# Memory-term loads two pieces ahead, its z vector only where it changes, and third-stage weights loaded three ahead

## The chip, the cores and the metric

The program runs on one NeuronCore of a Trainium2 chip. The metric is the device time of one execution in microseconds (us), shown as the median of three runs. A profiled execution of the same kernel gives the trace that the rows below are from.

## The reference

The inputs are q, k, v (4 batches x 8 heads x 576 tokens x 64), a memory matrix M per head (64 x 64), a vector z per head (64) and one gate value per head. Three stages follow one another:

```
a       = softmax(causal(q k^T / 8));  local = a v
qp      = phi(q),  phi(x) = x + 1 where x > 0, else exp(x)
mem     = (qp M) / (qp . z + 1e-6)
x       = g * mem + (1 - g) * local          g = sigmoid(beta), 2304 tokens x 512
x       = ((x w1) * (x w2)) w3 w_out         512 -> 1024 -> 1024 -> 512
h       = x w_in                             512 -> 2048
out     = (h - tanh(h)) w_out2               2048 -> 512
```

The weights arrive as 64-bit words and are decoded on the chip to fp32. Each matmul of the second and third stage is done three times over (high x high, high x low, low x high part of fp32), which is why a weight has a high and a low tile.

## The kernel before, in words

**First stage.** 16 head pairs, each in five blocks of queries: scores (`sc`), row maximum and exp (`st`, `p`), normalization on POOL, transposes (`t`, `g`), product with v (`o`), copied to the tiles `xs`. A background generator (`early`) is advanced a few steps per block: it folds w3 and w_out into one matrix (`fo`, `wf`), decodes the first weights of w1 and w2, and works on the memory term of the first group of tokens.

**Memory term.** The 2304 tokens are 18 pieces of 128, three to a group of 384. `mem_tok` works on one piece: load q (tile `mw`), min(q, 0) on DVE (L554), exp on ACT (L555), max(q, 0) plus that on DVE (L557), times z on POOL (L558), a reduction and a reciprocal on DVE (L561 to L564, tile `mst`), a scaling on POOL (L566), four transposes on PE (L570), and two copies to `mq` by the helper `copy`, which gives four in five to ACT (L438) and one to DVE (L440). `mem_mm` then multiplies `mq` by M, and DVE adds the result to `xs` (L587). z lies in one half of tile `mc` and is loaded anew for each piece (L552). Group 0 is worked on in the first stage, groups 1 to 5 in the second.

**Second stage.** Six groups g of 384 tokens, eight slices f each. For each (g, f): 24 matmuls with the weights `wa` and `wb` into two PSUM tiles `ab`; ACT copies one of them (`a`, L722); DVE multiplies (`a`, L723); ACT and DVE split the product into `abh` (L726) and `abl` (L727); 12 matmuls with `wf` for slice f - 1 (`x`). I write a(g,f) for the instruction of L723 of slice f of group g: it stands once per slice on DVE and serves as a clock of the stage. Between the slices steps of the memory term and of two decoders are put in. In group 0 the decoder `wd` supplies `wa` and `wb` slice by slice. After it the decoder `pre` takes the third stage's weights, in part: each of 24 pieces takes one load (L66), one ACT instruction (L74) and four DVE instructions (L75, L77, L81, L84), and ends in a tile named `z..p`. In group 5 a third decoder, `fd`, does the remaining eight pieces while the 24 are split into high and low.

A decoder has a width of two pieces being worked on at once, and a number `ahead` of pieces loaded or being worked on. The buffers of a load (`raw`) are three, those of the work (`T`) two.

**Third stage.** 96 slices: 12 matmuls (`h`), the function h - tanh(h) over ACT and DVE, 9 matmuls (`o`).

**Order.** The code yields between steps, and a scheduler in the build then puts the instructions of every engine and of the load queue (SP) in an order of its own. On the chip each engine runs its list in order, and so does SP: an instruction that waits holds up all behind it.

Of the kernel before, what the change touches and what calls it, by code (L numbers as in the profile page):

```python
# [11 lines left out]
F32 = mybir.dt.float32  # L12
# [5 lines left out]
AF = mybir.ActivationFunctionType  # L18
ALU = mybir.AluOpType
# [13 lines left out]
def block_kernel(ctx, tc, qk, qt, vt, mp, zp_d, beta, w1, w2, w3t, wo, wi, wo2, ident_d, mask_d, out):  # L33
    nc = tc.nc
    PE, DV, AC, PO, SP = nc.tensor, nc.vector, nc.scalar, nc.gpsimd, nc.sync
# [6 lines left out]
    zp = ctx.enter_context(tc.tile_pool(name="zp", bufs=1, side="right"))  # L42
# [104 lines left out]
    HIA, HF = 1, 1  # L147
# [7 lines left out]
    CLP = 0  # L155
# [19 lines left out]
    CPA = (0, 1, 3, 4)  # L175
# [125 lines left out]
    if True:  # L301
# [128 lines left out]
            AC.activation(out=dh, in_=src, func=AF.Copy)  # L430
            DV.tensor_tensor(out=dl, in0=src, in1=dh.bitcast(F32), op=ALU.subtract)

        ncopy = [0]

        def copy(dst, src, scale=None):
            ncopy[0] += 1
            if ncopy[0] % 5 in CPA:
                AC.activation(out=dst, in_=src, func=AF.Copy, scale=1.0 if scale is None else scale)  # L438
            elif scale is None:
                DV.tensor_copy(out=dst, in_=src)  # L440
            else:
                DV.tensor_scalar(out=dst, in0=src, scalar1=scale, scalar2=None, op0=ALU.mult)
# [56 lines left out]
        N = 384  # L499
# [19 lines left out]
        def ranges(t0, n):  # L519
            r = []  # L520
            t = t0
            while t < t0 + n:
                e = min(t0 + n, (t // 576 + 1) * 576)
                r.append((t - t0, e - t0, t // 576))
                t = e
            return r
# [7 lines left out]
        mem_t = {}  # L534

        def mem_setup():
            mem_t["c"] = zp.tile([128, 1024], F32, tag="z2", name="mc")
            mem_t["q"] = [zp.tile([128, 2, 512], F32, tag=f"z{3 + i}", name=f"mq{i}") for i in range(2)]
            mem_t["b"] = 0

        def mem_m(b):
            m = mem_t["c"][:, 512 + 256 * (b % 2):768 + 256 * (b % 2)]
            SP.dma_start(out=m.rearrange("p (a e) -> p a e", a=4), in_=mp[4 * b:4 * b + 4].rearrange("a p e -> p a e"))

        def mem_tok(g, tl):
            t0 = g * N + tl * 128
            w = zp.tile([128, 1024], F32, tag=f"z{tl % 2}", name="mw")
            qp, e_ = w[:, 0:512], w[:, 512:1024]
            SP.dma_start(out=qp, in_=qt[t0:t0 + 128])
            zb = mem_t["c"][:, 0:512]  # L550
            for a, e, b in ranges(t0, 128):
                SP.dma_start(out=zb[a:e], in_=zp_d[b:b + 1].squeeze(0).partition_broadcast(e - a))  # L552
            yield
            DV.tensor_scalar(out=e_, in0=qp, scalar1=0.0, scalar2=None, op0=ALU.min)  # L554
            AC.activation(out=e_, in_=e_, func=AF.Exp)  # L555
            yield
            DV.scalar_tensor_tensor(out=qp, in0=qp, scalar=0.0, in1=e_, op0=ALU.max, op1=ALU.add)  # L557
            PO.tensor_tensor(out=e_, in0=qp, in1=zb, op=ALU.mult)  # L558
            yield
            st = sm.tile([128, 24], F32, tag="mst", name="mst")  # L560
            DV.tensor_reduce(out=st[:, 0:8], in_=e_.rearrange("p (h d) -> p h d", h=8), axis=AX.X, op=ALU.add)  # L561
            DV.tensor_scalar(out=st[:, 8:16], in0=st[:, 0:8], scalar1=1e-6, scalar2=None, op0=ALU.add)
            DV.reciprocal(out=st[:, 16:24], in_=st[:, 8:16])
            DV.tensor_tensor(out=st[:, 0:8], in0=st[:, 16:24], in1=gates, op=ALU.mult)  # L564
            q3 = qp.rearrange("p (h d) -> p h d", h=8)
            PO.tensor_tensor(out=q3, in0=q3, in1=st[:, 0:8].unsqueeze(2).to_broadcast([128, 8, 64]), op=ALU.mult)  # L566
            yield
            t = ps["t"]()
            for hp in range(4):
                PE.transpose(t[:, hp * 128:hp * 128 + 128], qp[:, hp * 128:hp * 128 + 128], ident)  # L570
            for i in range(2):
                copy(mem_t["q"][i][:, :, tl * 128:tl * 128 + 128],
                     t[:, 256 * i:256 * i + 256].rearrange("p (a b) -> p a b", a=2))
            yield

        def mem_mm(g, i):
# [106 lines left out]
        pst.close()  # L683
        att.close()


        pools = {}
        for x in PO_:
# [17 lines left out]
        def ab_pe(xl, f):  # L706
            o = []
            for W in (W1, W2):
                p = psb.tile([128, 512], F32, tag="ab", name="ab")
                for k in range(4):  # L710
                    c = slice(k * 128, k * 128 + 128)
                    mm(p[:, 0:N], W[f][:, 0, c], xl[0][:, k], k == 0, False)
                    mm(p[:, 0:N], W[f][:, 0, c], xl[1][:, k], False, False)
                    mm(p[:, 0:N], W[f][:, 1, c], xl[0][:, k], False, k == 3)
                o.append(p)
            return o
# [3 lines left out]
        def ab_chain(g, f, o):  # L720
            a = b2.tile([128, N], F32, tag="a", name="a")
            AC.activation(out=a, in_=o[0][:, 0:N], func=AF.Copy)  # L722
            DV.tensor_tensor(out=a, in0=o[1][:, 0:N], in1=a, op=ALU.mult)  # L723
            h = b3.tile([128, N], F32R, tag="abh", name="abh")
            l = b3.tile([128, N], F32R, tag="abl", name="abl")
            AC.activation(out=h, in_=a, func=AF.Copy)  # L726
            DV.tensor_tensor(out=l, in0=a, in1=h[:].bitcast(F32), op=ALU.subtract)  # L727
            ab_t[g, f] = (h, l)
# [22 lines left out]
        def fslot(tag, dt=F32R):  # L751
            pool = zq if tag in ZX else xp if tag == "x0" else None
            return wslot(pool, tag, dt) if pool else slot(tag, dt)

        ftags = [*ZX, *ztags]
        NF = len(ftags)
        pre_t = {}

        def fin_src(j):
            f = j // 2  # L760
            return (wo2[f * 128:f * 128 + 128] if j % 2
                    else wi[:, f * 128:f * 128 + 128].rearrange("(k p) f -> p k f", p=128))

        def fin_item(j):
            def dst():
                t = fslot(free.popleft())
                fin_tiles[j] = t[:, 0], t[:, 1]
                return fin_tiles[j]

            return fin_src(j), dst  # L770

        def pre_item(j):
            def dst():
                i = j % NF
                if i not in pre_t:
                    pre_t[i] = fslot(ftags[i], F32)
                return pre_t[i][:, j // NF].bitcast(U32)

            return fin_src(j), dst
# [8 lines left out]
        def place(i, tags):  # L788
            for x, tag in enumerate(tags):
                t = fslot(tag)  # L790
                split(pre_t[i][:, x], t[:, 0], t[:, 1], DV if i % 3 == 2 else PO)
                fin_tiles[i + NF * x] = t[:, 0], t[:, 1]
            give([ftags[i]])

        wd = wdec[0]
        pre, fd, placed, left, plan = None, None, 0, [], list(PL)
# [3 lines left out]
        def give(tags):  # L800
            nonlocal given
            free.extend(tags)
            given += len(tags)
# [17 lines left out]
        for g in range(6):  # L821
            for f in range(8):
                wd.until(2 * f + 2)
                o = ab_pe(xl, f)
                ab_chain(g, f, o)
                if f >= 1:
                    x2_pe(g, f - 1)
                    if g == 5:
                        if f == 1:
                            pre.until(2 * NF)  # L830
                            fd = Decoder([fin_item(j) for j in range(2 * NF, 32)], 2, 2, PO if CLP else DV, False, HF)
                        left += [f"{x}{f - 1}" for x in ("wf", "wa", "wb")]
                        while plan and len(left) >= (2 if plan[0] == "P" else 1):
                            if plan.pop(0) == "P":
                                place(placed, [left.pop(0), left.pop(0)])
                                placed += 1
                            else:
                                give([left.pop(0)])
                    if g == 0:
                        wd.until(2 * f + 4)  # L840
                for _ in range(MS):
                    mem_step()
                if wd.done == 16:
                    if pre is None:
                        order = [*range(NZ), *range(NF, NF + NZ), *range(NZ, NF), *range(NF + NZ, 2 * NF)]
                        pre = Decoder([pre_item(j) for j in order], 2, 2, DV, True)
                    for _ in range(FS if g < 5 else FS5):
                        if pre.done < allowed:
                            pre.step()
                        elif fd and fd.done < given:  # L850
                            fd.step()
            if g + 1 < 6:
                mem_until(g + 1)
                xl = stage(g + 1)
            x2_pe(g, 7)
# [187 lines left out]
```

## Time and profile before

| | |
|---|---|
| time, three runs | 1062.58 us median (1062.35 to 1063.51) |
| profiled execution | 1063.58 us, its span 1061.8 us |
| mean granted TensorE clock | 0.976 of 2.4 GHz |
| PE matmul | 986.8 us busy, 93% of the span |
| PE weight loads | 862.6 us, 81% |
| DVE | 816.0 us, 77% |
| ACT | 614.4 us, 58% |
| POOL | 423.4 us, 40% |

Shares over the whole span hide that the stages have different limits. The first slice of the second stage reaches DVE at about 306 us, the second stage ends at about 657 us. A row is read from left to right: engine, line, operation, the tile that is written and those that are read; an idle time is put down to what ended it.

### The profile page before, as it was taken

The numbers are of one execution on the slowest core, as the hardware profiler recorded it, in microseconds if no ns is written. First come the engines' busy times: TensorE is split into PE (matmuls) and PEld (weight loads), VectorE is DVE, ScalarE is ACT, GpSimd is POOL, SyncE is SP. The second block draws the span as 40 slices with busy tenths as digits, with TensorE's granted clock in tenths as the row PEclk, the third lists the DMA queues.
The fourth block names the chain that finished last, engine by engine and source line by source line (L and its number), as shares of the span: only waits on it lengthen the run. The fifth ranks groups of instructions, "written<-read, shape, count | busy, mean of one in ns | idle before, by whom it ended". The sixth has DMA issues, their size and how long they took to land.

```text
span 1061.8 us, 15818 instructions
## 1 busy us (share of the span) xinstructions
PE 986.8 (93%) x5512; PEld 862.6 (81%) x5512; DVE 816.0 (77%) x1473; ACT 614.4 (58%) x1419; POOL 423.4 (40%) x432
## 2 busy tenths in 40 slices
PE   5799898978998898999999997999999999999998
PEld 3576666655687787999999997989999999999997
DVE  7989998999869998558221288788778788787776
ACT  5567677666732443334121444877777776776764
POOL 5888777777656422200000185322222222222221
PEclk9699999999999898999999999999999999999999
DMA  9764675552324454215000010000000000000000
GB/s 248 190 168 118 176 197 131 135 134 85 95 71 143 142 181 149 60 52 168 30 1 1 1 61 1 1 1 30 1 1 30 1 31 1 2 30 1 31 1 30
DMA packets 44415, 77.73 MB, mean 73 GB/s; under 512 B 5168, under 2 KB 30000, under 8 KB 42416
## 3 DMA queue, kind: packets, MB, share of 16 engines
q1 hardware_dynamic: 44336, 76.73, 25.7%
q8 instruction: 43, 0.70, 0.3%
q14 instruction: 36, 0.29, 0.1%
HBM read 72.00 MB, written 4.72 MB: 72 GB/s over the span
## 4 chain that ended last, share of the span: by engine, by line
PE 66%; DVE 21%; issue 4%; POOL 4%; ACT 2%; DMA 2%; SPq 0%; DVEq 0%; POOLq 0%; ACTq 0%
PE o L143 21%; PE h L143 19%; PE ab L143 13%; PE x L143 7%; DVE T L81 3%; DVE T L75 2%; PE sc L143 2%; POOL p L427 2%; DVE st L394 2%; DVE T L84 2%; PE fo L143 2%; DVE qs L224 2%; DVE T L77 2%; PE t L459 1%; DVE ks L226 1%
## 5 line engine op out<-in xcount | busy, mean ns | idle before, releaser
L925 POOL TENSOR_TENSOR gl<-s,gh 128x384 fp32r<-128x384 f32 x96 | 100.6, 1048 | 292.5 <-ACT gh L919 281.8
L427 POOL TENSOR_SCALAR p<-p,st 128x128 f32<-128x128 f32 (+2 forms) x144 | 111.7, 787 | 55.1 <-DVE st L420 25.8
L143 PE MATMUL x<-abh,wf 128*128 128x384 f32 x384 | 110.5, 349 | 4.1 <-ACT abh L726 4.1
L143 PE MATMUL ab<-xh,wa 128*128 128x384 f32 x384 | 110.3, 345 | 4.0 <-DVE a L723 2.0
L143 PE MATMUL ab<-xh,wb 128*128 128x384 f32 x384 | 108.4, 340 | 2.9 <-POOL wb L96 2.0
L143 PE MATMUL sc<-ks,qs 128*128 128x256 f32 (+4 forms) x384 | 91.7, 358 | 18.5 <-DVE qs L224 9.5
L407 ACT ACTIVATE p<-sc,st 128x256 f32<-128x256 f32 (+4 forms) x160 | 82.5, 527 | 32.6 <-DVE st L394 13.3
L901 DVE SCALAR_TENSOR_TENSOR s<-s,u 128x384 f32<-128x384 f32 x96 | 82.0, 855 | 22.0 <-ACT s L891 21.0
L723 DVE TENSOR_TENSOR a<-ab,a 128x384 f32<-128x384 f32 x48 | 26.4, 551 | 85.8 <-PE ab L143 73.0
L74 ACT ACTIVATE T<-raw 128x512 f32<-128x512 f32 x72 | 48.7, 677 | 67.8 <-POOL wa L99 14.0
L897 ACT ACTIVATE u<-u,pc 128x384 f32<-128x384 f32 x96 | 59.3, 619 | 43.6 <-DVE s L901 43.5
L143 PEld LDWEIGHTS sc<-ks,qs 128*128 128x128 f32 x384 | 63.0, 205 | 26.1 <-ACT p L407 10.1
L907 DVE TENSOR_TENSOR t<-h,t 128x384 f32<-128x384 f32 x96 | 53.3, 555 | 38.1 <-ACT t L890 37.7
L143 PEld LDWEIGHTS ab<-xh,wa 128*128 128x128 f32 x384 | 71.2, 191 | 8.8 <-issue 3.2
L143 PEld LDWEIGHTS x<-abh,wf 128*128 128x128 f32 x384 | 72.8, 195 | 5.3 <-ACT abh L726 5.0
L459 PE MATMUL t<-ident,p 128*128 128x128 f32 x320 | 54.7, 292 | 22.4 <-DVE g L440 8.1
L889 ACT ACTIVATE u<-h 128x384 f32<-128x384 f32 x96 | 47.0, 490 | 47.2 <-PE h L143 47.2
L143 PEld LDWEIGHTS ab<-xh,wb 128*128 128x128 f32 x384 | 71.2, 191 | 3.9 <-POOL wb L96 2.3
L143 PE MATMUL x<-abl,wf 128*128 128x384 f32 x192 | 67.9, 354 | 4.2 <-DVE abl L727 4.2
L906 DVE SCALAR_TENSOR_TENSOR s<-s,s 128x384 f32<-128x384 f32 x96 | 61.3, 638 | 8.5 <-DVE s L901 0.9
L143 PE MATMUL ab<-xl,wa 128*128 128x384 f32 x192 | 65.6, 341 | 0.0
L913 DVE COPY_PREDICATED s<-u,t 128x384 f32<-128x384 uint32 x96 | 58.5, 610 | 8.6 <-ACT t L890 0.5
(228 smaller groups left out, 2796.6 us busy)
## 6 DMA issues: line engine op xcount, KB each, us to landing
r<-in_qk SPq DMA_DIRECT2D x30, 576.0 KB, 7.4
raw<-in_wo SPq DMA_DIRECT2D x24, 512.0 KB, 3.6
raw<-in_w3t SPq DMA_DIRECT2D x16, 512.0 KB, 4.8
raw<-in_w SPq DMA_DIRECT2D x16, 512.0 KB, 3.6
raw<-in_wi SPq DMA_DIRECT2D x16, 512.0 KB, 3.8
v<-in_vt SPq DMA_DIRECT2D x16, 320.0 KB, 6.6
mw<-in_qt SPq DMA_DIRECT2D x18, 256.0 KB, 3.1
out<-ob SPq DMA_DIRECT2D x18, 256.0 KB, 2.3
```

The lines of the kernel that those rows point to most:

```text
L74: AC.activation(out=tf, in_=hw.bitcast(F32), func=AF.Abs)
L143: return PE.matmul(o, lhsT, rhs, start=start, stop=stop).ins
L407: mark["A"][n] = AC.activation(out=p_t[n][:, o:o + w], in_=sc_t.pop((n, x))[:, 0:w], func=AF.Exp, bias=st[:, b:b + 1], accum_out=st[:, 2 + ...
L427: (DV if NV[u] == "V" else PO).tensor_scalar(out=pr, in0=pr, scalar1=sc, scalar2=1.0, op0=ALU.mult, op1=ALU.mult)
L459: PE.transpose(t[:, m], p[:, K * h + 128 * kb:K * h + 128 * kb + 128], ident)
L889: AC.activation(out=u, in_=o, func=AF.Square)
L897: AC.activation(out=u, in_=u, func=AF.Relu, bias=pc[:, 2:3])
L901: DV.scalar_tensor_tensor(out=s1, in0=s1, scalar=k2[0], in1=u, op0=ALU.add, op1=ALU.mult)
L906: DV.scalar_tensor_tensor(out=s1, in0=s2, scalar=k2[1], in1=s1, op0=ALU.add, op1=ALU.mult)
L907: DV.tensor_tensor(out=t, in0=o, in1=t, op=ALU.subtract)
L913: DV.copy_predicated(out=s1, mask=u[:].bitcast(U32), data=t)
L925: PO.tensor_tensor(out=l, in0=s1, in1=h[:].bitcast(F32), op=ALU.subtract)
```

## The change

Four edits. (1) The load of q is taken out of `mem_tok` into `mem_q`: pieces 0 and 1 are loaded at the start, piece i + 2 after the copies of piece i. One yield per piece goes with it. (2) The load of z is taken into `mem_z`, called after the product with z of the piece before, and issues only where the batch changes: 8 loads in place of 20. (3) From the end of the first stage on (`late`), the minimum is taken by ACT as relu(-q), whose negative goes into the exp, and all copies to `mq` are on ACT. (4) `pre` and `fd` have up to three pieces ahead in place of two.

```
-            if ncopy[0] % 5 in CPA:
+            if late[0] or ncopy[0] % 5 in CPA:
...
+        def mem_q(i):
+            if i < 18:
+                w = mem_t["w"][i] = zp.tile([128, 1024], F32, tag=f"z{i % 2}", name="mw")
+                SP.dma_start(out=w[:, 0:512], in_=qt[128 * i:128 * i + 128])
+
+        def mem_z(i):
+            new = [(a, e, b) for a, e, b in ranges(128 * i, 128)] if i < 18 else None
+            if new and (i == 0 or new != ranges(128 * i - 128, 128)):
+                for a, e, b in new:
+                    SP.dma_start(out=mem_t["c"][a:e, 0:512], in_=zp_d[b:b + 1].squeeze(0).partition_broadcast(e - a))
...
-            SP.dma_start(out=qp, in_=qt[t0:t0 + 128])
             zb = mem_t["c"][:, 0:512]
-            for a, e, b in ranges(t0, 128):
-                SP.dma_start(out=zb[a:e], in_=zp_d[b:b + 1].squeeze(0).partition_broadcast(e - a))
-            yield
-            DV.tensor_scalar(out=e_, in0=qp, scalar1=0.0, scalar2=None, op0=ALU.min)
-            AC.activation(out=e_, in_=e_, func=AF.Exp)
+            if late[0]:
+                AC.activation(out=e_, in_=qp, func=AF.Relu, scale=-1.0)
+                AC.activation(out=e_, in_=e_, func=AF.Exp, scale=-1.0)
+            else:
+                DV.tensor_scalar(out=e_, in0=qp, scalar1=0.0, scalar2=None, op0=ALU.min)
+                AC.activation(out=e_, in_=e_, func=AF.Exp)
             yield
             DV.scalar_tensor_tensor(out=qp, in0=qp, scalar=0.0, in1=e_, op0=ALU.max, op1=ALU.add)
             PO.tensor_tensor(out=e_, in0=qp, in1=zb, op=ALU.mult)
+            mem_z(i + 1)
...
+            mem_q(3 * g + tl + 2)
...
+        late[0] = True
...
-                            fd = Decoder([fin_item(j) for j in range(2 * NF, 32)], 2, 2, PO if CLP else DV, False, HF)
+                            fd = Decoder([fin_item(j) for j in range(2 * NF, 32)], 2, 3, PO if CLP else DV, False, HF)
...
-                        pre = Decoder([pre_item(j) for j in order], 2, 2, DV, True)
+                        pre = Decoder([pre_item(j) for j in order], 2, 3, DV, True)
```

The scheduler makes a new order of it on every engine. On DVE, in group 1, from the decoding of the tile `zAp` to the a(g,f) behind the second `z5p`: before (a(1,2) is the last row),

```order
L84 SCALAR_TENSOR_TENSOR zAp<-raw,T 128x512
L77 TENSOR_SCALAR T<-T 128x512
L81 SCALAR_TENSOR_TENSOR T<-raw,T 128x512
L75 TENSOR_SCALAR T<-T 128x512
L84 SCALAR_TENSOR_TENSOR zBp<-raw,T 128x512
L77 TENSOR_SCALAR T<-T 128x512
L554 TENSOR_SCALAR mw<-mw 128x512
L81 SCALAR_TENSOR_TENSOR T<-raw,T 128x512
L84 SCALAR_TENSOR_TENSOR z5p<-raw,T 128x512
L557 SCALAR_TENSOR_TENSOR mw<-mw 128x512
L723 TENSOR_TENSOR a<-ab,a 128x384
```

and in the changed kernel, from `zBp` on (a(1,2) is L740 there, L557 is L571, L564 is L579):

```order
L84 SCALAR_TENSOR_TENSOR zBp<-raw,T 128x512
L579 TENSOR_TENSOR mst<-mst,gates 128x8
L77 TENSOR_SCALAR T<-T 128x512
L81 SCALAR_TENSOR_TENSOR T<-raw,T 128x512
L75 TENSOR_SCALAR T<-T 128x512
L84 SCALAR_TENSOR_TENSOR z5p<-raw,T 128x512
L77 TENSOR_SCALAR T<-T 128x512
L740 TENSOR_TENSOR a<-ab,a 128x384
L571 SCALAR_TENSOR_TENSOR mw<-mw 128x512
```

The minimum (L554) is gone from DVE, the decoding keeps its place, and the sum with the exp (L557, now L571) stands behind a(1,2).

On ACT, in group 1, around three slices: before,

```order
L438 ACTIVATE mq_1783<-mo 128x2x128
L438 ACTIVATE mq_1784<-mo 128x2x128
L722 ACTIVATE a<-ab 128x384
L555 ACTIVATE mw<-mw 128x512
L726 ACTIVATE abh<-a 128x384
L722 ACTIVATE a<-ab 128x384
```

and in the changed kernel (L565 is the new relu, L566 the exp, L739 and L743 the former L722 and L726):

```order
L438 ACTIVATE mq_1783<-mo 128x2x128
L438 ACTIVATE mq_1784<-mo 128x2x128
L565 ACTIVATE mw<-mw 128x512
L566 ACTIVATE mw<-mw 128x512
L739 ACTIVATE a<-ab 128x384
L438 ACTIVATE mq_1783<-mo 128x2x128
L438 ACTIVATE mq_1784<-mo 128x2x128
L743 ACTIVATE abh<-a 128x384
```

The relu stands directly ahead of the copy `a` that the slice needs, and waits for the load of q.

On SP, where the third stage's first weights are loaded (`in_wi`, `in_wo`): before,

```order
L66 DMA raw<-in_wi 128x4x128
L549 DMA mw<-in_qt 128x512
L66 DMA raw<-in_wo 128x512
L549 DMA mw<-in_qt 128x512
L66 DMA raw<-in_wi 128x4x128
L552 DMA mc<-in_zp 128x512
L66 DMA raw<-in_wo 128x512
L549 DMA mw<-in_qt 128x512
```

and in the changed kernel:

```order
L66 DMA raw<-in_wi 128x4x128
L66 DMA raw<-in_wo 128x512
L547 DMA mw<-in_qt 128x512
L66 DMA raw<-in_wi 128x4x128
L557 DMA mc<-in_mp 128x4x64
L66 DMA raw<-in_wo 128x512
L547 DMA mw<-in_qt 128x512
L66 DMA raw<-in_wi 128x4x128
```

The loads of z are gone from between the weights, and each load of q is for a piece later than the one that is next.

## Rows read from the trace of the kernel before

**Rows 1.** Windows by stretch: engines' busy us (instructions), granted clock, DMA share, GB/s

```profile
0.00:306.57 306.57, 255.70 (x1647) 184.50 (x1648) 273.68 (x566) 202.00 (x567) 223.88 (x257) 0.96 0.57 147
306.57:418.68 112.11, 100.19 (x544) 89.54 (x541) 107.06 (x194) 41.55 (x82) 45.29 (x37) 0.94 0.49 154
418.68:479.25 60.57, 59.41 (x354) 56.78 (x356) 32.32 (x72) 19.12 (x41) 13.10 (x11) 0.97 0.22 63
617.00:657.00 40.00, 33.83 (x179) 32.23 (x179) 38.94 (x44) 17.19 (x32) 28.94 (x23) 0.96 0.13 41
```

**Rows 2.** Timeline of DVE: start us, us, instruction, idle before it

```profile
306.57 0.56 DVE L723 TENSOR_TENSOR a<-ab,a 128x384 f32<-128x384 f32 x1 [0.48 <-ACT a L722]
...
418.68 0.55 DVE L723 TENSOR_TENSOR a<-ab,a 128x384 f32<-128x384 f32 x1
...
510.36 0.56 DVE L723 TENSOR_TENSOR a<-ab,a 128x384 f32<-128x384 f32 x1 [4.33 <-PE ab L143]
...
516.64 0.56 DVE L723 TENSOR_TENSOR a<-ab,a 128x384 f32<-128x384 f32 x1 [4.57 <-PE ab L143]
```

**Rows 3.** Waits of PE from 300 to 430: total us, times, longest

```profile
PE x L143 <- ACT abh L726: 4.1, 3, 1.9
PE ab L143 <- POOL wb L96: 2.0, 1, 2.0
```

**Rows 4.** Groups of DVE instructions, 306.57 to 418.68: count, busy us, mean ns, idle before

```profile
L81 DVE SCALAR_TENSOR_TENSOR T<-raw,T 128x512 uint16<-128x512 uint32 x26 | 21.7, 841 | 0.3
L77 DVE TENSOR_SCALAR T<-T 128x512 uint32<-128x512 uint32 x26 | 16.0, 614 | 0.1
...
L557 DVE SCALAR_TENSOR_TENSOR mw<-mw 128x512 f32<-128x512 f32 x9 | 6.8, 760 | 0.0
...
L561 DVE TENSOR_REDUCE mst<-mw 128x8 f32<-128x512 f32 x8 | 5.4, 675 | 1.2 <-POOL mw L558 1.2
L554 DVE TENSOR_SCALAR mw<-mw 128x512 f32<-128x512 f32 x9 | 3.8, 421 | 1.7 <-DMA mw<-in_qt 1.7
L562 DVE TENSOR_SCALAR mst<-mst 128x8 f32<-128x8 f32 x7 | 2.5, 364 | 0.0
...
L440 DVE COPY mq<-mo 128x256 f32<-128x256 f32 x4 | 1.6, 410 | 0.0
L564 DVE TENSOR_TENSOR mst<-mst,gates 128x8 f32<-128x8 f32 x7 | 1.5, 215 | 0.0
...
L563 DVE RECIPROCAL mst<-mst 128x8 f32<-128x8 f32 x7 | 1.3, 192 | 0.0
```

**Rows 5.** Waits of DVE in the same stretch

```profile
DVE mw L554 <- DMA mw<-in_qt: 1.7, 2, 1.0
DVE T L75 <- ACT T L74: 1.5, 3, 0.5
```

**Rows 6.** Waits of ACT from 300 to 430

```profile
ACT abh L726 <- DVE a L723: 10.5, 7, 2.8
...
ACT T L74 <- DMA raw<-in_wi: 7.8, 4, 2.8
```

**Rows 7.** Groups of ACT instructions from 300 to 430

```profile
L555 ACT ACTIVATE mw<-mw 128x512 f32<-128x512 f32 x10 | 6.3, 633 | 16.6 <-DVE mw L554 13.9 <-DVE mst L562 2.7
L438 ACT ACTIVATE mq<-mo 128x256 f32<-128x256 f32 x16 | 5.4, 377 | 8.7 <-PE mo L570 7.1 <-DVE mq L440 1.6
```

**Rows 8.** Waits over the whole span: DVE for q, and SP's own

```profile
DVE mw L554 <- DMA mw<-in_qt: 14.2, 8, 4.2
...
SPq L552 <- POOL mw L558: 43.5, 15, 8.2
```

**Rows 9.** Instructions on tile T, 305 to 420, then L81 from 430: ns min/median/max

```profile
L75 DVE TENSOR_SCALAR T<-T x26: 386/424/1397, 308.7 to 415.7; 128x512 f32<-128x512 f32 x26
...
L81 DVE SCALAR_TENSOR_TENSOR T<-raw,T x10: 735/756/765, 468.2 to 502.9; 128x512 uint16<-128x512 uint32 x10
```

**Rows 10.** Instructions on tile mw, 306.57 to 418.68

```profile
L554 DVE TENSOR_SCALAR mw<-mw x9: 406/423/435, 309.9 to 411.6; 128x512 f32<-128x512 f32 x9
```

More of the change, by code (lines that the diff above doesn't have):

```diff
@@ L431, in evac @@
             DV.tensor_tensor(out=dl, in0=src, in1=dh.bitcast(F32), op=ALU.subtract)
-        ncopy = [0]
+        ncopy, late = [0], [False]
         def copy(dst, src, scale=None):
             ncopy[0] += 1
-            if ncopy[0] % 5 in CPA:
+            if late[0] or ncopy[0] % 5 in CPA:
                 AC.activation(out=dst, in_=src, func=AF.Copy, scale=1.0 if scale is None else scale)
@@ L538, in mem_setup @@
             mem_t["q"] = [zp.tile([128, 2, 512], F32, tag=f"z{3 + i}", name=f"mq{i}") for i in range(2)]
-            mem_t["b"] = 0
+            mem_t["b"], mem_t["w"] = 0, {}
+            mem_q(0)
+            mem_z(0)
+            mem_q(1)
+        def mem_q(i):
[7 more added lines that the diff above has]
+                    SP.dma_start(out=mem_t["c"][a:e, 0:512], in_=zp_d[b:b + 1].squeeze(0).partition_broadcast(e - a))
         def mem_m(b):
@@ L545, in mem_tok @@
         def mem_tok(g, tl):
-            t0 = g * N + tl * 128
-            w = zp.tile([128, 1024], F32, tag=f"z{tl % 2}", name="mw")
+            i = 3 * g + tl
+            w = mem_t["w"].pop(i)
             qp, e_ = w[:, 0:512], w[:, 512:1024]
-            SP.dma_start(out=qp, in_=qt[t0:t0 + 128])
             zb = mem_t["c"][:, 0:512]
-            for a, e, b in ranges(t0, 128):
-                SP.dma_start(out=zb[a:e], in_=zp_d[b:b + 1].squeeze(0).partition_broadcast(e - a))
-            yield
-            DV.tensor_scalar(out=e_, in0=qp, scalar1=0.0, scalar2=None, op0=ALU.min)
-            AC.activation(out=e_, in_=e_, func=AF.Exp)
+            if late[0]:
[4 more added lines that the diff above has]
+                AC.activation(out=e_, in_=e_, func=AF.Exp)
             yield
```

## The prediction

> **What bounds the kernel now.** I read the windows by stretch first. In the first stage, up to 306.57 us, DVE is busy for 273.68 us and PE for 255.70. From 306.57 to 418.68 DVE is busy for 107.06 of 112.11 us and PE for 100.19 [rows 1]; from 418.68 to 479.25 it is the reverse, PE 59.41 of 60.57 us and DVE 32.32. From 617 to 657 DVE is full again, 38.94 of 40 [rows 1]. So one engine has to be relieved in one stretch: DVE, in groups 0 and 1 of the second stage.
>
> The timeline says how far that stretch is from what PE could do. Once nothing is late, a(g,f) comes every 516.64 - 510.36 = 6.28 us, and DVE then waits for PE [rows 2]. Between a(0,1) at 306.57 and a(1,5) at 418.68 lie 12 slices in 112.1 us, 9.3 us each. PE's idle there is 112.11 - 100.19 = 11.9 us, and the granted clock is 0.94, so some time was spent at 1.2 GHz: 6% of full rate lost, 6.7 us. These two, 18.6 us, bound what can be won here. The waits of PE name late results of the slices (`x` for `abh`, 4.1 us) and late weights [rows 3]; `abh` in turn waits for DVE's product, 10.5 us [rows 6]. DVE itself sits idle for only 5 us. Hence a(1,5) comes when DVE has worked off what stands ahead of it in its list, and counting that list is the way to a number.
>
> **The change, part by part.** I counted DVE's instructions between a(0,1) and a(1,5) in both orders. Both have 12 a, 13 `abl`, 12 additions to `xs`, 26 of L75, and as many decoded ends (L84). The change takes away 9 minima at 421 ns (3.8 us), 4 copies at 410 (1.6), one L81 at 841 and one L77 at 614 (1.5): 6.9 us [rows 4]. The scheduler puts one more piece of the memory term into the stretch: one more L557 (760 ns), one reduction (675), three additions of 1e-6 (364 each), two reciprocals (192) and two products (215): 3.3 us [rows 4]. DVE's own gain is 3.5 us, not the 6.3 that 15 minima in the whole second stage would suggest.
>
> Next the stalls. DVE waits 1.7 us for q and 1.5 us for ACT's first step of a decoded piece [rows 5], which itself waited for third-stage weights, 7.8 us up to 430 [rows 6]. Loads two pieces and three pieces ahead take both away: bounds 0 and 3.2 us, and I take 3.2, because the order of SP puts the q loads a piece earlier and drops z loads, which had held SP for 43.5 us behind POOL in all [rows 8]. The larger part of DVE's 14.2 us of waiting for q [rows 8] lies where PE is full, and is worth nothing.
>
> So a(1,5) comes 6.7 us earlier. What remains for PE from there is the same in both orders: the slices, and two groups of memory matmuls (8 additions to `xs` follow in each). But the decoding of the third stage has moved forward: between a(1,5) and a(2,5) stand 88 DVE instructions in place of 71. At the mean of the loaded stretch, 107.06/194 = 0.55 us each, and with its idle share (112.11/107.06), they take 51 us, where the old kernel took 60.57 us with PE as the limit [rows 1]. The cover is about 10 us, and it should hold: behind 430 us an L81 takes 756 ns and at most 765 [rows 9], against 841 in the loaded stretch [rows 4]. But the decoding stands in clumps, the longest 17 instructions between a(2,1) and a(2,2), 17 x 0.55 = 9.4 us where a slice has 6.28. Bounds: 0, and 3 us, the excess of that clump; I take 1.
>
> The ACT side costs nothing as long as ACT is not the limit: it is busy for 41.55 of 112.11 us [rows 1]. A relu of the size of the exp, 633 ns, for each of 9 or 10 pieces, and 4 copies at 377 [rows 7], add about 8 us to that. z loads cost nothing on POOL's side either way. `fd` with three ahead: DVE is full from 617 to 657 [rows 1] with the same list before and after, so an earlier load meets an engine that has no time for it: 0. The first stage gets a new order, too, with the same number of DVE instructions ahead of a(0,0) (565) and the same kinds but for one or two; there I take 0, with bounds of 3 us either way, 1% of its 306.57 us.
>
> Sum: -3.5 - 3.2 + 1.0 = -5.7. From the profiled execution's 1063.58 that is 1057.9 us. The median of the runs lies 1.0 below that execution, so 1056.9 us.
>
> A rule to weigh. Decode steps on DVE are stretched: L75 takes 424 ns in the median and up to 1397, while the minima take 406 to 435 [rows 9, 10]. The Trainium skill (SBUF - State Buffer, Who interferes with whom) says that DVE in a two-port mode and GpSimd lock each other out for a whole instruction, whichever comes second. By it the minima that go were not those that were blocked (the trace agrees: 406 to 435), and the extra piece's two POOL instructions may block two decode steps by up to 1397 - 424 = 1.0 us each. The sum would be -3.7 instead of -5.7, and the time 1058.9. No run here shows two such kernels apart.
>
> **The rivals.**
>
> *It gains more.* The lower clock level is met where PE has its idle time; if the idle goes, so may the 6.7 us lost at 1.2 GHz. For it: the next stretch, with PE nearly full, was granted 0.97 against 0.94 [rows 1]. Against: of 107 us of DVE's load here 103.5 stay. 1056.9 - 6.7 = 1050.2 us.
>
> *No change.* The order of the first stage, where DVE is busy for 273.68 of 306.57 us [rows 1], is new from the folding's second half on. A loss there of up to 2% (6 us) eats the gain, or the decoder's chain of ACT, DVE and POOL with two `T` tiles sets its own pace, so that DVE idles where the minima were. Against: the number of instructions ahead of a(0,0) is unchanged, and DVE hardly idles now. About 1062.6 us.
>
> *Slower.* Relu now waits for q on ACT, in front of the copy `a` without which the slice's product can't start; before, DVE waited, ahead of decoding that could bear it. If q comes late as often as now, 14.2 us over 8 pieces, 1.8 us each [rows 8], and does so for 8 of the 15 late pieces, ACT, then DVE, then PE lose 14 us, of which those in the stretch bound by DVE count, two thirds: 9.5 us. With the 6.7 us won and the 1.0: 1062.6 - 6.7 + 1.0 + 9.5 = 1066.4 us. It decides from 5.7 us in all on, 0.6 us for each of the 10 pieces in the stretch. For it: SP runs in order, and a q load behind a weight load whose buffer isn't free comes late however early it was written. Against: a whole piece of work lies between load and use.
>
> **How the numbers follow.** The forecast has 0.52, the greater gain 0.10, no change 0.18, slower 0.20. The forecast's own range goes from all bounds in its favour (-6.7 and -3 of the first stage: 1052.9) to all against (0 for the stalls, 3 for clumps: 1062.6 - 3.5 + 3 = 1062.1); most of it is below 1060.4, that is, faster by over 0.2%, about 2.1 us, below which a measurement can't tell a change. Its tail above I count as no change. Faster: 0.62; same 0.18; slower 0.20. The range for 8 in 10 reaches from 1049.5, which takes in the greater gain, to 1066.5, which takes in the slower case's middle.
>
> **What would show it.** In the new profile: a(1,5) about 112.1 - 6.7 = 105.4 us behind a(0,1); no wait of DVE or ACT for `in_qt` over 0.5 us; a(2,5) within 61 us of a(1,5); the stretch from a(3,1) to the end unchanged to 1 us, and a(0,1) at 306.6 within 3 us. The forecast is wrong if ACT's relu shows waits for q in groups 0 and 1 of more than 6 us in all, if DVE stays above 95% busy up to a(2,5), or if a(0,1) itself moves by more than 3 us.

## The result, and the profile after

The changed kernel takes 1071.27 us (median of four runs, 1069.93 to 1074.11) against 1062.46 for the kernel before (four runs, 1062.11 to 1063.51): 1.0085 times as long, with a 95% interval of 1.0063 to 1.0106. It is slower, and outside the range. The profiled execution is the longest of the four, 1074.11 us, with a span of 1072.3 and a granted clock of 0.968.

The windows by stretch, of the kernel after. They answer to [rows 1]; the second starts with a(0,1) and ends with a(1,5), the third ends with a(2,5).

```profile
0.00:314.57 314.57, 262.51 (x1648) 188.63 (x1648) 274.20 (x566) 204.07 (x571) 224.10 (x255) 0.92 0.56 142
314.57:428.72 114.15, 99.75 (x552) 88.61 (x552) 107.31 (x190) 49.68 (x100) 53.88 (x43) 0.96 0.46 143
428.72:489.94 61.22, 60.08 (x349) 55.98 (x350) 44.70 (x90) 22.13 (x46) 7.11 (x6) 0.97 0.32 97
627.00:667.00 40.00, 33.81 (x179) 32.19 (x178) 38.94 (x44) 17.15 (x32) 28.90 (x23) 0.96 0.13 41
```

The first stretch is 314.57 us long in place of 306.57. DVE does 274.20 us of work in it, against 273.68: nearly all of the 8 us is idle time of DVE. The second is 114.15 in place of 112.11 us where 105.4 was forecast, and DVE is busy for as long as before, 107.31 us. The fourth has the same load as before (38.94 of 40 us).

The timeline of DVE at its a rows, kernel after ([rows 2]; the first row holds a(0,0) and a(0,1), the third is a(3,1)):

```profile
314.11 1.01 DVE L740 TENSOR_TENSOR a<-ab,a 128x384 f32<-128x384 f32 x2
...
428.72 0.54 DVE L740 TENSOR_TENSOR a<-ab,a 128x384 f32<-128x384 f32 x1
...
513.99 0.56 DVE L740 TENSOR_TENSOR a<-ab,a 128x384 f32<-128x384 f32 x1 [1.11 <-PE ab L143]
```

a(3,1) came at 504.33 us before. So of the 10.5 us by which the span grew, 8.0 stand at a(0,1), 2.0 more at a(1,5), -0.4 by a(3,1), and 0.9 behind it: about three quarters of the loss have arisen by the end of the first stage, and the gain never came in the second.

The last exp of the first stage, on the timeline of ACT, of the kernel before:

```profile
285.42 0.51 ACT L407 ACTIVATE p<-sc,st 128x256 f32<-128x256 f32 x1
```

And of the kernel after:

```profile
297.74 0.47 ACT L407 ACTIVATE p<-sc,st 128x256 f32<-128x256 f32 x1
```

It is 12.3 us later. What came ahead of it are the multiplications of the memory term's first group, `mem_mm`: tile mo, 206 to 298 us, kernel after (ns min/median/max, first and last start, forms).

```profile
L143 PE MATMUL mo<-mq,mc x16: 482/483/533, 288.1 to 295.6; 64*64 64x384 f32 x16
L603 DVE TENSOR_TENSOR xs<-mo,xs x4: 547/550/558, 289.7 to 297.6; 128x384 f32<-128x384 f32 x4
```

Before, the first such matmul is at 288.6, behind the last exp. And five reductions of pieces stand ahead of the last exp in place of three. Tile mst, kernel after:

```profile
L576 DVE TENSOR_REDUCE mst<-mw x5: 658/676/686, 212.6 to 295.0; 128x8 f32<-128x512 f32 x5
```

Tile mst, kernel before:

```profile
L561 DVE TENSOR_REDUCE mst<-mw x3: 670/674/675, 217.8 to 271.3; 128x8 f32<-128x512 f32 x3
```

From the first exp of head pair 10 (187.43 us before, 188.86 after) to the last exp DVE has 31 memory instructions of 13.4 us in place of 20 of 9.1, and PE is busy for 5.5 us with 28 memory matmuls and transposes in place of 1.5 us with 11. That first exp is already 1.4 us late with the same instructions of PE and DVE ahead of it, so 6.6 of the 8.0 us arise behind it.

The clock may have a share in this. The windows from that first exp to the last one, of the kernel before:

```profile
187.43:285.42 97.99, 81.83 (x563) 57.86 (x560) 95.11 (x205) 68.65 (x198) 73.31 (x85) 0.98 0.44 119
```

And of the kernel after:

```profile
188.86:297.74 108.88, 91.97 (x582) 62.92 (x580) 99.71 (x218) 72.18 (x207) 78.26 (x88) 0.91 0.40 107
```

PE is busy for 10.1 us more, of which the memory term accounts for 4.0, and the granted clock is 0.91 in place of 0.98, so more of the time was spent at 1.2 GHz. PE also idles more (16.9 us in place of 16.2). No run tells how much of the delay the lower clock causes and how much it follows from.

Groups of DVE from a(0,1) to a(1,5): first L75 of the kernel before (its L81 and L77 are in [rows 4], 841 and 614 ns),

```profile
L75 DVE TENSOR_SCALAR T<-T 128x512 f32<-128x512 f32 x26 | 15.3, 590 | 1.5 <-ACT T L74 1.5
```

then the kernel after:

```profile
L81 DVE SCALAR_TENSOR_TENSOR T<-raw,T 128x512 uint16<-128x512 uint32 x25 | 23.4, 936 | 0.2
L75 DVE TENSOR_SCALAR T<-T 128x512 f32<-128x512 f32 x26 | 16.6, 637 | 5.0 <-ACT T L74 5.0
L77 DVE TENSOR_SCALAR T<-T 128x512 uint32<-128x512 uint32 x25 | 16.3, 652 | 0.2
...
L571 DVE SCALAR_TENSOR_TENSOR mw<-mw 128x512 f32<-128x512 f32 x10 | 6.8, 676 | 0.1
```

The minima and copies are gone, and the list is shorter, as counted; but the three decode steps take 56.3 us against 53.0. The wait of L75 for ACT, 1.5 us before [rows 5], is 5.0. Waits of ACT from 300 to 430, first the kernel before, then the kernel after:

```profile
ACT T L74 <- POOL wa L99: 12.9, 5, 5.8
```

```profile
ACT T L74 <- POOL wa L99: 14.5, 4, 5.2
...
ACT mw L565 <- DMA mw<-in_qt: 6.2, 5, 2.0
```

ACT's decode step L74 waits longest for POOL to release a `T`, but it did so before (the prediction took only its 7.8 us for weights). Behind the four waits of L75 stand others: once a relu (L565) that waits for q, and three times third-stage weights that L74 waits for. The longest, on ACT and on DVE, kernel after:

```profile
317.96 0.63 ACT L565 ACTIVATE mw<-mw 128x512 f32<-128x512 f32 x1 [1.32 <-DMA mw<-in_qt]
318.50 0.66 ACT L74 ACTIVATE T<-raw 128x512 f32<-128x512 f32 x1
```

```profile
319.18 1.53 DVE L75 TENSOR_SCALAR T<-T 128x512 f32<-128x512 f32 x1 [2.15 <-ACT T L74]
```

Waits of PE from 300 to 430 ([rows 3]):

```profile
PE x L143 <- ACT abh L743: 5.1, 2, 3.7
PE x L143 <- DVE abl L744: 3.5, 3, 1.6
PE ab L143 <- POOL wa L99: 2.5, 2, 1.2
```

PE still waits for the slices' results, more than before.

### The profile page after: what moved, and what is told of

It is laid out like the page before. It is cut to its first block, busy times and chain, and to the rows that moved or that the text cites. A ratio compares the mean times of both kernels' runs of the same rounds, so it can differ in the third digit from the quotient of the medians.

```text
span 1072.3 us, 15790 instructions
## 1 busy us (share of the span) xinstructions
PE 993.0 (93%) x5512; PEld 865.3 (81%) x5512; DVE 812.4 (76%) x1452; ACT 623.3 (58%) x1440; POOL 426.3 (40%) x432
## 4 chain that ended last, share of the span: by engine, by line
PE 60%; DVE 7%; issue 2%; ACT 1%; DMA 1%; POOL 0%; DVEq 0%; POOLq 0%; ACTq 0%
PE o L143 19%; PE h L143 19%; PE ab L143 14%; PE x L143 7%; DVE T L81 2%; DVE T L75 1%; DVE T L77 1%; PE mo L143 1%; DVE abl L744 1%; DVE T L84 0%; DMA raw<-in_wi 0%; DVE a L740 0%; DVE mst L576 0%; DVE xl L720 0%; PE mo L585 0%
## 5 line engine op out<-in xcount | busy, mean ns | idle before, releaser
L427 POOL TENSOR_SCALAR p<-p,st 128x128 f32<-128x128 f32 (+2 forms) x144 | 114.4, 807 | 56.8 <-DVE st L420 29.9
L74 ACT ACTIVATE T<-raw 128x512 f32<-128x512 f32 x72 | 48.6, 675 | 82.8 <-POOL wa L99 16.2
L740 DVE TENSOR_TENSOR a<-ab,a 128x384 f32<-128x384 f32 x48 | 26.4, 552 | 91.1 <-PE ab L143 83.9
L81 DVE SCALAR_TENSOR_TENSOR T<-raw,T 128x512 uint16<-128x512 uint32 x72 | 65.9, 915 | 0.7
```

The lines of the kernel that those rows point to most:

```text
L74: AC.activation(out=tf, in_=hw.bitcast(F32), func=AF.Abs)
L81: DV.scalar_tensor_tensor(out=l16, in0=lw, scalar=2.0 ** -29, in1=l16, op0=ALU.mult, op1=ALU.add)
L427: (DV if NV[u] == "V" else PO).tensor_scalar(out=pr, in0=pr, scalar1=sc, scalar2=1.0, op0=ALU.mult, op1=ALU.mult)
```

## Experiments

One part of the change gives nothing to test: with `ahead` set back to 2, the order of the instructions on all five engines and on SP is the same as with 3, in either kernel. That was read from the orders; no run was made. The theory of the first runs: the loss comes from the early q loads together with the lost yield, by way of the order, not from ACT.

The yield's arithmetic: a piece of group 0 has four steps in place of five, the group 3 x 4 + 2 = 14 in place of 17. At the end of the background list each step is followed by two of the weights', three yields per step, 42 in place of 51, while `BG` steps per block stayed. In the second stage `MS` = 4 steps go between two slices, so a piece passes in one slice, not in 5/4.

**1. Early q, with and without the yield, and the ACT edits alone** (all on the kernel before).

```
 # e1_q_no_yield: mem_q as in the change, and
-            yield
             DV.tensor_scalar(out=e_, in0=qp, ... op0=ALU.min)
```

> The kernel before with the early loads of q alone, and with them the yield per piece gone; z, minimum, copies and loads ahead as before. Theory 1 (the missing yield moves the background work of the first stage forward and gives that stage a worse order): a(0,1) 5 to 8 us later than the 306.6 of before, the whole 5 to 8 us slower (about 1069). Theory 2 (ACT's relu waits for q and holds ACT): nothing of that is in this kernel, so within 2 us of before. Theory 3 (q loads that wait for a buffer hold the load queue ahead of the weights): slower by 3 us or more, but with a(0,0) to a(1,5) longer, not a(0,1) later.

```
 # e2_q_with_yield: mem_q as in the change, the yield stays
+                w = mem_t["w"][i] = zp.tile([128, 1024], F32, tag=f"z{i % 2}", name="mw")
+                SP.dma_start(out=w[:, 0:512], in_=qt[128 * i:128 * i + 128])
...
             yield
             DV.tensor_scalar(out=e_, in0=qp, ... op0=ALU.min)
```

> As the one before, with the yield kept, so that the steps of the first stage fall as before. Theory 1: a(0,1) within 2 us of 306.6, the whole within 2 us of before or up to 3 us faster by the waits for q that go. Theory 2: within 2 us. Theory 3: slower by 3 us or more, as in the other kernel.

```
 # e3_late_only
+            if late[0]:
+                AC.activation(out=e_, in_=qp, func=AF.Relu, scale=-1.0)
+                AC.activation(out=e_, in_=e_, func=AF.Exp, scale=-1.0)
 # and every copy to mq on ACT
```

> The kernel before with the relu on ACT and all copies of the memory term on ACT after the first stage; loads as before. Theory 1: a(0,1) within 2 us of before, the whole 0 to 6 us faster, since DVE loses 15 minima and some copies. Theory 2: ACT waits for q where DVE did (14 us over 8 pieces), a(1,5) comes later behind a(0,1) than the 112.1 us of before, the whole 3 to 8 us slower. Theory 3: within 3 us.

```
 # e4_after_early_yield: kernel after, and ahead of the relu and the minimum
+            if g < EM:
+                yield
```

> The changed kernel with the yield put back for the three pieces of group 0 alone, so that the first stage is advanced as before; all else as changed. Theory 1: a(0,1) back within 2 us of 306.6, the whole about 6 us faster than the changed kernel (1065). Theory 2: no faster than 1070. Theory 3: no faster than 1070.

Against 1061.41 us for the kernel before in these runs: e1 1070.28, 1.0095 [1.0071, 1.012]; e2 1061.31, 0.9999 [0.9984, 1.0014]; e3 1060.99, 0.9988 [0.9976, 1.0001]; e4 1064.8, 1.0028 [1.0016, 1.0039]. (Behind each median stands its ratio to the kernel before, with the 95% interval.) Early loads cost nothing and bring nothing; with the yield gone as well, the whole loss is there, with no relu in the kernel. At a(0,1) it is less than expected, 3.0 us late (309.59) in place of 5 to 8. In e3's profile the stretch up to a(1,5) takes 109.10 us, 3.0 less than before, DVE's work 1.9 of it (105.15 us); the whole is not shown to be faster. e4 regains about two thirds of the loss: its last exp is at 285.54 and a(0,1) at 308.41.

Why early loads bring nothing, the waits show. Waits for q over the whole span, e2 (before: 14.2 us, [rows 8]):

```profile
DVE mw L560 <- DMA mw<-in_qt: 13.8, 9, 3.5
```

And SP's own waits from 300 to 500 us, first before, then e2:

```profile
SPq L549 <- PE mo L570: 36.7, 8, 10.4
```

```profile
SPq L546 <- PE mo L576: 38.1, 9, 14.7
```

The tile `mw` has two buffers, and the load of piece i + 2 goes into that of piece i. So SP waits until PE has transposed piece i, and the load, though written earlier, starts no earlier: from the fourth piece on, 2.2 to 5.2 us lie between its issue and the minimum in e2, 2.3 to 5.4 us in the kernel before (from the timelines).

**2. The yield alone, in both directions.**

```
 # e5_after_all_yields: kernel after, and ahead of "if late[0]"
+            yield
 # e6_before_no_yield_group0: kernel before
-            yield
+            if g >= EM:
+                yield
 # e7_before_no_yield_late: kernel before
-            yield
+            if g < EM:
+                yield
 # e8_before_second_yield_group0: kernel before, ahead of the minimum
             yield
+            if g < EM:
+                yield
```

> The changed kernel with the yield put back for all 18 pieces: early loads, z only where it changes, relu and copies on ACT, three ahead. Theory 1 (the missing yield is what costs, in both stages): a(0,1) near 307, and a(0,1) to a(3,1) shorter than with the yield in group 0 alone (197.2 us) by about 5 us, the whole about 1058 (the early loads alone gave 194.5 for that stretch, ACT's relu alone 193.2, before 197.8). Theory 1b (the yield matters in the first stage alone): about 1064.8, as with the yield in group 0 alone. Theory 2 (ACT's relu or the z edit costs): 1064 or more.

> The kernel before with nothing changed but the yield taken out for the three pieces of group 0, loads as before. Theory 1: a(0,1) 3 to 8 us late, the memory term's DVE time ahead of the last exp up from 9.1 us to about 14, the whole 3 to 8 us slower (1065 to 1069). Rival (the early loads or their place on the load queue cost in the first stage, not the yield): within 2 us of before.

> The kernel before with nothing changed but the yield taken out for the pieces of groups 1 to 5. Theory 1: a(0,1) within 1 us of 306.6, a(0,1) to a(3,1) 2 to 5 us longer than the 197.8 of before, the whole 2 to 5 us slower. Theory 1b: within 1.5 us of before.

> The kernel before with one yield more for the three pieces of group 0, so that its memory term comes later in the first stage. If memory work ahead of the last exps is what costs (by its size), this is no slower than before up to a(0,1), perhaps 1 to 3 us faster, with less than 9.1 us of it ahead of the last exp. If any new order of the first stage costs, since its other numbers go with five steps, it is 3 us slower or more.

Against 1062.31: e5 1059.76, 0.9976 [0.9957, 0.9996]; e6 1067.34, 1.0049 [1.003, 1.0068]; e7 1080.79, 1.017 [1.0136, 1.0204]; e8 1067.48, 1.0047 [1.0032, 1.0063]. e6 and e7 differ from the kernel before by a yield only, and are slower. In e6 the delay shows late: a(0,1) is at 308.07, 1.5 us late where 3 to 8 were expected, and a(0,2) at 321.63, 5.5 us late. e7 is 18 us slower where 2 to 5 were expected. Tile mo of e6, 206 to 294 us:

```profile
L143 PE MATMUL mo<-mq,mc x16: 482/482/533, 284.3 to 290.9; 64*64 64x384 f32 x16
```

The last exp of e6, on the timeline of ACT:

```profile
292.74 0.47 ACT L407 ACTIVATE p<-sc,st 128x256 f32<-128x256 f32 x1
```

So the 16 matmuls stand ahead of the last exp, which comes 7.3 us later than before: the picture of the changed kernel, without one of its four edits. e8 puts memory work later instead, its last exp is at 285.16, and it loses all the same (a(0,1) at 311.88). The minimum that stands on DVE ahead of the additions to `xs` tells where; before, and in e8:

```profile
288.66 0.43 DVE L554 TENSOR_SCALAR mw<-mw 128x512 f32<-128x512 f32 x1 [1.94 <-DMA mw<-in_qt]
```

```profile
297.17 1.05 DVE L556 TENSOR_SCALAR mw<-mw 128x512 f32<-128x512 f32 x1 [4.97 <-DMA mw<-in_qt]
```

In e8 it waits 5.0 us for a q whose load starts only at 292.97, when PE has transposed the piece in that buffer. The additions that group 0's first products need stand behind it, and from there to a(0,0) at 311.30 DVE idles for 0.2 us, where it had 5.2 us to spare ahead of a(0,0) before. So memory work that comes too early holds up the last exps, and memory work that comes too late holds up what group 0 needs.

For e7 the second stage tells; waits of PE from 300 to 520 us, e7:

```profile
PE x L143 <- ACT abh L727: 10.7, 4, 3.1
PE mo L571 <- POOL mw L567: 8.8, 4, 2.5
```

With four steps of a four-step piece in each slice PE meets transposes whose piece POOL hasn't scaled. DVE waits too, for q; waits of DVE from 300 to 450, e7:

```profile
DVE mw L555 <- DMA mw<-in_qt: 11.6, 7, 3.2
```

**3. The pace by other means, and what remains of the edits.**

```
 # e9_after_early_yield_ms3: e4, and
-    MS, FS, FS5 = 4, 3, 6
+    MS, FS, FS5 = 3, 3, 6
 # e10_after_padded_steps: kernel after; 9 empty steps over the 14 of the list's end
-            a = early_w()
+            a, k = early_w(), 0
             while a or b:
...
+                k += 1
+                if k <= 14 and k % 14 % 3 != 1:
+                    yield
 # e11_q_and_late_with_yields: e5 without mem_z; z is loaded with each piece
-            mem_z(i + 1)
+            for a, e, b in ranges(128 * i, 128):
+                SP.dma_start(out=zb[a:e], in_=zp_d[b:b + 1].squeeze(0).partition_broadcast(e - a))
 # e12_z_only: kernel before with mem_z
+            mem_z(3 * g + tl + 1)
```

> The changed kernel with the yield put back for group 0 (as measured before: 1064.8), and in the second stage three steps of the memory term per slice (MS 3) in place of four, so that a piece of four steps goes at 3/4 of a piece per slice, near the 4/5 of before. If the yield mattered through the pace (pieces too dense for DVE ahead of the slices): a(0,1) near 307, a(0,1) to a(3,1) back from 197.2 to 194 or below, the whole about 1060, level with all yields put back (1059.8). If the point between load and use mattered instead, or any order but the old one costs: no better than 1064.

> The changed kernel (no yield in a piece) with nine empty yields spread over the 14 memory steps of the first stage, so that the background there takes 51 yields over group 0 as before, in other places. If pace alone is what costs in the first stage: last exp near 285.5 and a(0,1) near 307, the whole about 1065, like the yield put back for group 0. If the order at the level of single steps matters (the second yield for group 0 cost 5 us although the work came later): a(0,1) 3 us late or more, the whole 1067 to 1071.

> The kernel with all yields put back, and z loaded for every piece as in the kernel before: early q, relu and copies on ACT. If the z edit is worth something by freeing the load queue: 1 to 3 us slower than with it (1059.8), so 1061 to 1063. If it is worth nothing: within 1 us of 1059.8.

> The kernel before with z loaded only where the batch changes, all else as before. First stage the same order up to its end, so a(0,1) within 1 us of before. The load queue's waits for the product with z go (23.5 us from 300 on), but the weights it delays are not what DVE waits for: within 1.5 us of before; if it mattered, 1.5 to 4 us faster.

Against 1062.98: e9 1060.99, 0.998 [0.9966, 0.9994]; e10 1063.44, 1.0 [0.9987, 1.0013]; e11 1057.21, 0.9951 [0.9938, 0.9963]; e12 1063.37, 1.0008 [0.9995, 1.0021]. e10 has all four edits and no work more or less than the changed kernel, only 9 empty steps, and in time nearly all of the loss is gone: so the loss hangs on where the background's steps fall, not on the work of the edits. e9 came as expected in time, and its a(0,1) to a(3,1) takes 194.69 us. The last exp of e10:

```profile
289.03 0.50 ACT L407 ACTIVATE p<-sc,st 128x256 f32<-128x256 f32 x1
```

Its tile mo (the first ten of the 16 matmuls): they start behind that exp.

```profile
L143 PE MATMUL mo<-mq,mc x10: 482/482/533, 291.2 to 293.9; 64*64 64x384 f32 x10
```

By its own expectation e10 is a mixed answer: the last exp is 3.6 us late and a(0,1), at 310.11, 3.5 us, which was to be the sign that single steps matter, while the whole is faster than either theory said. At a(3,1) e10 is 8.3 us ahead of the changed kernel, and only 4.5 of these are there at a(0,1). The rest comes in the second stage, whose code is the same as in the changed kernel and in e4, but not its order on the engines. The windows from a(0,1) to a(1,5), e10, then e4:

```profile
310.11:417.76 107.65, 94.73 (x548) 84.68 (x546) 102.64 (x185) 47.74 (x98) 49.50 (x42) 1.00 0.48 147
```

```profile
308.41:420.71 112.30, 99.08 (x529) 89.59 (x528) 105.13 (x190) 47.45 (x95) 47.84 (x38) 0.89 0.47 146
```

The pace, the order that the scheduler makes of it and the granted clock (1.00 against 0.89) change together here, and no run separates them.

e11 missed its expectation: without the z edit the kernel is no slower. It is faster by 0.9976 - 0.9951 = 0.25% or about 2.6 us, but the two intervals overlap (e5 0.9957 to 0.9996, e11 0.9938 to 0.9963), so a cost of the z edit is not shown, and e12 shows that edit alone at no change. The profile of e12 has a(0,1) 2.0 us late, at 308.54, where 1 us was allowed; its head pair 10 already starts late (see the last section).

**4. The second stage's pace on top.** The question of these two runs is whether the slices' pace alone explains the second stage.

```
 # e13_after_pad_and_ms3: e10, and        # e14_before_no_late_yield_ms3: e7, and
-    MS, FS, FS5 = 4, 3, 6
+    MS, FS, FS5 = 3, 3, 6
```

> The changed kernel, no yield put back in any piece: nine empty yields over the 14 memory steps of the first stage, and three memory steps per slice in the second. If pace is the whole cause: the whole about 1060 (1071.3, less 7.8 by the padding, less 3.8 by the three steps, and not under 1059), faster than before. If the point of the yield between load and use matters, too: 1063 or more.

> The kernel before without the yield in groups 1 to 5 (1080.8, 18 us slower than before) and three memory steps per slice. If pace is the cause there, too: within 4 us of before (1062 to 1067). If it is that a load of q now has no step between it and its use, so that DVE waits for it: 1075 or more, with over 8 us of DVE's waits for q from 300 to 450.

Against 1063.25: e13 1063.24, 1.0001 [0.9987, 1.0015], a miss, as it should have gained some 3 us over e10 (its expectation kept 1063 or more for the case that the point of the yield counts, too); e14 1055.48, 0.9935 [0.9913, 0.9957]. e14 is e7 with three steps per slice in place of four, 25 us faster than it, and the fastest of all kernels here: faster than the kernel before by 0.65% with none of the four edits, and faster than either theory said. The kernel before with three steps and all its yields was not run. The windows of e14 from a(0,1) to a(1,5):

```profile
306.44:409.52 103.08, 93.80 (x527) 84.45 (x525) 99.06 (x181) 39.19 (x79) 43.71 (x36) 0.98 0.48 154
```

The same of e7:

```profile
309.46:432.53 123.07, 100.73 (x530) 90.73 (x529) 108.99 (x204) 40.86 (x80) 47.30 (x39) 0.90 0.47 147
```

And of e11:

```profile
306.45:414.71 108.26, 96.10 (x547) 87.14 (x545) 105.34 (x188) 47.14 (x95) 46.94 (x39) 0.97 0.52 163
```

e7 has 204 instructions of DVE ahead of a(1,5), e14 has 181 (before: 194): the pace decides how much of the memory term stands in the stretch that DVE bounds, and how much comes where PE is full. PE's waits for `abh` from 300 to 520 us, e14:

```profile
PE x L143 <- ACT abh L727: 2.0, 1, 2.0
PE mo L571 <- POOL mw L567: 1.4, 1, 1.4
```

DVE's waits for q from 300 to 450 us, e14 (11.6 in e7):

```profile
DVE mw L555 <- DMA mw<-in_qt: 7.6, 5, 3.4
```

Three steps per slice have a price, too: a(2,5) to a(3,1) takes 30.0 to 30.2 us in e9, e13 and e14, and 23.9 to 25.1 in all others. It is paid back where the stretches ahead of it get shorter by more: a(0,1) to a(1,5) by 6.0 us from e4 to e9 and by 20.0 from e7 to e14, but not from e10 (107.65) to e13 (108.80), where that stretch was already short.

## Why the prediction was wrong

**The step that failed** is that on the first stage: "there I take 0, with bounds of 3 us either way". It rested on the number of DVE instructions ahead of a(0,0). That number is right (566 records in either trace, 274.20 us against 273.68), but it says nothing on where the last exps stand among them. The change's "One yield per piece goes with it" was read as nothing; it is the cost. In place of 0, a(0,1) came 8.0 us late, and e1 and e2, which differ by the yield alone, stand at 1.0095 and 0.9999. By the ratios, the yield of group 0 is worth 1.0085 - 1.0028 = 0.57%, 6 us, and that of the later groups 1.0028 - 0.9976 = 0.52%, 5.5 us. These are no fixed prices: in the kernel before the later yields are worth 1.7% (e7), and e10 regains the 0.85% without either. Two of the prediction's own signs of error appeared: a(0,1) moved by over 3 us, and the relu waited for q for more than 6 us (below). The forecast's own range, too, took this term's 3 us on one side only: with +3 against it, its upper end is 1065.1 in place of 1062.1, still short of 1071.27.

**DVE's list, -3.5, and the stalls, -3.2.** These failed as well: in the changed kernel the stretch is 2.0 us longer, not 6.7 shorter. The minima and copies went, as counted, but DVE stayed busy for as long (decode steps +3.3 us). Its idle time in the stretch went from 5.05 to 6.84 us, and L75's wait grew by 3.5 us, where it was forecast to vanish. The stalls' term had the loads wrong: three ahead changes no instruction's place, and the early q load starts only when its buffer is free (e2). So the wait for q did not go, it moved from DVE to ACT. With the yields kept the sizes are not borne out either. The windows from a(0,1) to a(1,5), e5:

```profile
306.65:417.96 111.31, 97.50 (x546) 86.73 (x545) 106.51 (x188) 47.21 (x95) 47.16 (x39) 0.95 0.46 145
```

All four edits with all yields (e5) gain 0.24% (0.04 to 0.43), 2.5 us, and this stretch is 0.8 us shorter than before. Without the z edit (e11) the gain is 0.49% (0.37 to 0.62), 5.2 us, near the 5.7 of the sum; but in its profile, 6.9 us shorter than that of before, DVE's work in the stretch fell by 1.7 us and its idle time by 2.1, and another 3.1 us came between a(1,5) and a(3,1), which the sum doesn't have. That the total is near is in part luck.

**The rule weighed**, by the Trainium skill (SBUF — State Buffer, Who interferes with whom), that DVE in a two-port mode and GpSimd lock each other out, speaks for the direction: POOL is busy for 53.88 us in the stretch in place of 45.29, and the means of L75 and L77, the decode steps with a single input tile, rose from 590 and 614 ns to 637 and 652. That it is the cause is not shown: no row tells which of them ran in such a mode, and in e11, with POOL at 46.94 us, L75 takes 664 ns and L77 554. Groups of DVE from a(0,1) to a(1,5), e11:

```profile
L81 DVE SCALAR_TENSOR_TENSOR T<-raw,T 128x512 uint16<-128x512 uint32 x26 | 26.5, 1018 | 0.2
L75 DVE TENSOR_SCALAR T<-T 128x512 f32<-128x512 f32 x26 | 17.3, 664 | 0.1
L77 DVE TENSOR_SCALAR T<-T 128x512 uint32<-128x512 uint32 x26 | 14.4, 554 | 0.2
```

**The clumps, +1.0.** a(2,5) is 61.22 us behind a(1,5) (60.57 before): +0.65, within the term's bounds. DVE is busy for 73% there, so the cover held.

**`fd` and the end, 0.** From a(3,1) to the end 558.31 us against 557.45, within the 1 us given. That three ahead does nothing is sharper than the prediction put it: no instruction moved.

**ACT's side, 0, and the rival "slower".** ACT's relu waits for q for 7.9 us from a(0,0) to a(1,7), that is, in groups 0 and 1, over the 6 given as its mark. Waits of ACT from 314 to 447 us, kernel after:

```profile
ACT mw L565 <- DMA mw<-in_qt: 7.9, 6, 2.0
```

The prediction held against it that "a whole piece of work lies between load and use"; in the trace 2.2 to 4.3 us lie between the issue of a load and its relu. So what the rival feared occurs, and one wait of 2.15 us on DVE is traced to it above. But it doesn't explain the loss: e11 has the relu with waits of the same size (7.3 us from 300 to 430, against 6.2 in the changed kernel) and is faster, and e1 has the loss without a relu. Waits of ACT from 300 to 430 us, e11:

```profile
ACT mw L567 <- DMA mw<-in_qt: 7.3, 6, 2.4
```

The rival "no change" named the first stage's new order; that is the larger part of the loss, at 8 us of the traces in place of its 6, and without the gain that was to balance it. The rival "it gains more" asked for a higher clock in the second stage: it rose from 0.94 to 0.96 up to a(1,5), and the stretch got no shorter.

**z, 0.** Alone that held (e12); a cost together with the rest is not shown (e11).

Still open: how much of the loss is the pace itself, how much the order that the scheduler makes of it, and how much the clock; why the changed kernel's second stage gains 3.8 us from empty steps in the first (e10); whether the z edit costs in company. In all of these the instructions' order is new throughout, and a trace of one order doesn't tell which of its many changes counts.

## What to carry to other kernels

Where steps of background work are counted out per block or slice, a yield is part of the schedule: an edit that removes one changes the pace of all that follows, and the constants tuned to it have to be set anew. Before a forecast, set the old and the new order side by side at the end of each stage and ask what stands ahead of the last instructions that the next stage needs; a count of instructions up to the end does not show it. To judge an edit, run it once with the pace held as it was (here 0.9976 with the yields, e5, against 1.0085 without). And before a load is written earlier, ask when its buffer comes free: with two buffers, the load for the piece after next waits for the piece at hand.

## What the runs showed of the hardware

The first exp of head pair 10 came between 187.1 and 190.0 us over the profiled executions, with the same instructions of PE and DVE ahead of it (only some loads of q and z stand elsewhere): a spread of 3 us, as large as some of the effects told here, which follows none of the edits. Hence the totals above, not single milestones, carry the verdicts. The mean decode step L81 in the stretch from a(0,1) to a(1,5) lay between 804 ns (e8) and 1018 ns (e11) for one and the same instruction, and it did not follow POOL's busy time (45.43 and 46.94 us there, 53.88 us with 936 ns in the changed kernel).
